# The second transform stage with 128 weight columns per matmul instead of two matmuls of 64

## The chip, the cores and the metric

The kernel runs on one core of a Trainium2 chip. The metric is the device time of one execution, in microseconds (us). Before the change three runs gave 624.28, 624.87 and 624.88 us, median 624.87.

## What is computed

The model is one block with two branches, each behind a layer norm whose scale and shift come from a small conditioning vector. The first branch is a long convolution along the sequence (2048 positions, 512 channels), the second a feed-forward layer with a squared ReLU. Cut to what matters here:

```
K  = real(einsum("dn,dnl,dn->dl", C, exp(dt*A*l), dt*B))   # 512 channels, 2048 taps
Kf = rfft(pad(K, 2048));  Uf = rfft(pad(h.T, 2048))
y  = irfft(Uf * Kf)[:2048].T + h * Dskip
x  = x + ga * y
x  = x + gb * (relu(layernorm(x)*(1+cb)+sb) @ w1 + b1)**2 @ w2 ...
```

The kernel never calls an FFT: both transforms, of the filter K and of the input u, are products with constant matrices, in two stages. The change touches the second of them.

## The kernel before

The 512 channels are cut into 8 chunks of 64 (`NC = 8`), and each chunk passes through the same steps twice, once for the input (lower-case u below) and once for the filter that the kernel generates:

- *Filter generation* (lines around 730 to 805): ScalarE makes sines and exponentials, GpSimd and VectorE multiply them into factors, and TensorE contracts them into a bank called `kg` (line 804, weights of 32 columns).
- *Stage 1* (`stage1`, line 668): a transform of length 32, as matmuls with 64 weight columns and 128 moving columns; the two halves `r` of the output, real and imaginary, go to the two halves of the 128 partitions of a PSUM bank.
- *Stage 2* (`stage2`, line 678): for each of the 32 frequencies k1 a transform of length 64 over the 128 partitions. The weight is `t2_sb[:, k1, r]`, 64 columns for each half r; the moving operand is a strided slice of 64 columns of a 2048-column spectrum tile (called `xy`). One call handles 8 values of k1 and fills one bank `ps`, and one chunk needs four calls. Eight chunks, input and filter, four calls each: 64 calls, 16 matmuls each, 1,024 matmuls in all.
- *Product and first inverse stage* (lines 814, 823, 829): VectorE multiplies the filter's spectrum, straight from the PSUM bank of stage 2, with the input's; TensorE then applies `e1_sb` (64 weight columns, 128 moving).
- *Second inverse stage* (line 1016, weights of 32 by 32), layer norm, and the feed-forward layer (lines 1090 to 1134), whose matmuls have 128 weight columns and 512 moving columns of a rounded 32-bit type.

Every one of these transform matmuls is in plain 32-bit floats, and the profile shows two weight loads and two matmul records for each. So a call of stage 2 leaves 32 records of each kind before the change, in the form 128*64 128x64: weights of 128 rows by 64 columns, 64 moving columns.

The banks `ps` are three, handed round in turn (`PS, XY = 3, 7`). ScalarE empties the input's banks of stage 2 (line 701), and VectorE the filter's (line 814).

The order of the work is not the order of the code. `keep_order` walks all recorded instructions with a model of each engine's time and gives every engine a fixed list. Its time for a plain matmul depends on the number of weight columns:

```python
            tiles = 128 // cols if cols in (32, 64, 128) else 1
            t = max(1.7 * moving / tiles, 116 / tiles)
```

and it adds 100 ns whenever the number of weight columns on TensorE changes from one group to the next. In this model two matmuls of 64 columns with 64 moving columns take 2 x 58 = 116 ns, and so does one of 128 columns. It also keeps a modelled clock of TensorE, and a count of instruction words (`length`, 4 for a plain 32-bit matmul) after which the next block of instructions must have been fetched. Pieces of work also carry hand-set priorities (`HURRY`).

Of the kernel before, what the change touches and what calls it, by code (L numbers as in the profile page):

```python
# [320 lines left out]
def tile_adaln_ssm_ffn(  # L321
# [18 lines left out]
    nc = tc.nc  # L340
# [24 lines left out]
    def bank(tag, bufs, shape=None):  # L365
        n = 1024 if tag == "tg" else 512
        t = ring(psum, tag, bufs, [P, n])
        if shape is None:
            return t
        names = "abcd"[: len(shape) - 1]  # L370
        return t.rearrange(f"p ({' '.join(names)}) -> p {' '.join(names)}", **{x: v for x, v in zip(names, shape[1:])})
# [20 lines left out]
    def held(pool, slot, name, shape, dt=F32):  # L392

        t = pool.tile(shape, dt, tag=slot, name=name)
        slots[t.tensor.name] = slot
        return t
# [19 lines left out]
    def runs(xs):  # L416
        return xs.rearrange("p d m t -> p (d m t)")
# [24 lines left out]
    t2_sb = held(ka, "t2", "t2_sb", [P, 32, 2, 64])  # L442
# [171 lines left out]
    for row_, v in ((g1, g4), (s1, s4)):  # L614
        for q in range(4):
            nc.tensor.matmul(
                row_[:, 128 * q : 128 * q + 128], ident[:, 32 * q : 32 * q + 1].to_broadcast([P, P]), v,
                start=True, stop=True)
# [53 lines left out]
    def stage2(xs, g):  # L672

        ps = bank("ps", PS)
        src = runs(xs).rearrange("p (q k h t) -> p k q h t", q=16, h=2, t=2)
        for i in range(8):
            for r in range(2):
                nc.tensor.matmul(  # L678
                    ps[64 * r : 64 * r + 64, 64 * i : 64 * i + 64].rearrange("p (h q t) -> p q h t", h=2, t=2),
                    t2_sb[:, 8 * g + i, r], src[:, 8 * g + i], start=True, stop=True)  # L680
        return ps.rearrange("p (k h q t) -> p h q k t", k=8, h=2, t=2)


# [11 lines left out]
    def u_pieces(c):  # L695
        xs = xus[c] = spectrum()
        for g in range(4):
            stage1(x_sb[c][:, 4 * g : 4 * g + 4], xs, 4 * g)
            yield
        for g in range(4):  # L700
            nc.scalar.copy(piece(xs, g), stage2(xs, g))
            yield
# [105 lines left out]
    def product_pieces(c):  # L808
        xu, sw, xk = xus[c], sws[c], xks[c]
        yr, yu = spectrum(), spectrum()  # L810
        for g in range(4):
            ps = stage2(xk, g)
            for y, x in ((yr, sw), (yu, xu)):
                nc.vector.tensor_mul(product_piece(y, g), ps, piece(x, g))  # L814
            if g == 3:
                spectra.extend((sw, xu, xk))
            yield
        for g in range(4):
            ps = bank("ps", PS)
            for i in range(4):  # L820
                for h, y in ((0, yu), (1, yr)):
                    for m in range(2):
                        nc.tensor.matmul(  # L823
                            ps[64 * m : 64 * m + 64, 128 * i : 128 * i + 128],
                            pairs(y)[:, g, i // 2, 64 * m : 64 * m + 64, i % 2],
                            e1_sb[:, h], start=(h == 0), stop=(h == 1))
            copy = nc.vector.tensor_copy
            for r in range(2):
                copy(z4[r][c][:, :, 4 * g : 4 * g + 4], ps.rearrange("p (d r j) -> p j d r", d=4, r=2)[..., r])  # L829
            if g == 3:  # L830
                spectra.extend((yr, yu))
            yield
# [493 lines left out]
```

## Time and profile before

| What | Value |
|---|---|
| Median of three runs | 624.87 us |
| Span of the profiled execution | 625.9 us (the page gives no other time for it; 1.0 us over the median) |
| Matmuls busy (PE) | 566.7 us, 9,230 records |
| Weight loads busy (PEld) | 490.4 us, 9,230 records |
| VectorE, ScalarE, GpSimd busy | 485.4, 425.1, 251.7 us |
| Stage 2 (line 678), matmuls | 66.8 us busy, 2,048 records, between 75.7 and 282.6 us of the span |

The columns of a group of instructions are its line, engine and operation, output and inputs by name, the shape of the weights (rows*columns), the shapes of output and moving operand, the count, then busy time in us and the mean duration of one in ns, and then the idle time before them with what ended it. PE rows are matmuls, PEld rows the weight loads that go with them; a matmul's duration includes the passage through the array, so records of one stream overlap, and the distance between their starts is what the stream costs. In the chain of waits each row is a start, a length and the work that the end of the program depended on in that time.

### The profile page before, as it was taken

How to read it: one execution, taken by the hardware profiler on the slowest of the kernel's cores; microseconds unless marked ns; L12 is line 12 of the kernel's file. 1: busy time of each engine (PE TensorE's matmuls, PEld its weight loads, DVE VectorE, ACT ScalarE, POOL GpSimd, SP SyncE). 2: the span in 40 equal slices, each digit the busy share in tenths (PEclk: the TensorE clock that was granted, in tenths of full speed). 3: DMA queues.
4: the chain of work that ended last, by engine and by line, in shares of the span. 5: the costliest groups of instructions: out<-in, count | busy, mean ns of one | idle time of the engine just before them, and what ended most of it. 6: DMA issues, size and time to landing. Idle time of an engine off the chain costs nothing.

```text
span 625.9 us, 21088 instructions
## 1 busy us (share of the span) xinstructions
PE 566.7 (91%) x9230; PEld 490.4 (78%) x9230; DVE 485.4 (78%) x846; ACT 425.1 (68%) x752; POOL 251.7 (40%) x215
## 2 busy tenths in 40 slices
PE   1338999999999999989699899999999999999996
PEld 1236889899899998988578678888888878888885
DVE  3999968798699979835898998646999886655744
ACT  2966879989989677641575866757666766666530
POOL 3849699899998898471004100000000500000000
PEclk9999999999999999999689999999999999999999
DMA  9940231130303303156206421112521532111432
GB/s 319 398 146 3 70 70 31 45 71 3 72 5 71 67 7 71 31 125 225 85 4 214 147 78 34 35 34 85 186 84 45 174 102 72 47 34 35 144 96 79
DMA packets 31355, 57.00 MB, mean 91 GB/s; under 512 B 4512, under 2 KB 13600, under 8 KB 29856
## 3 DMA queue, kind: packets, MB, share of 16 engines
q1 hardware_dynamic: 30832, 55.53, 29.2%
q8 instruction: 72, 1.18, 0.8%
q10 hardware_dynamic: 432, 0.14, 0.1%
q14 instruction: 19, 0.16, 0.1%
HBM read 43.07 MB, written 4.19 MB: 76 GB/s over the span
## 4 chain that ended last, share of the span: by engine, by line
PE 60%; DVE 18%; ACT 12%; DMA 4%; issue 4%; POOL 0%; SPq 0%; DVEq 0%; ACTq 0%
PE ps L668 7%; PE ps L678 7%; PE ps L823 7%; PE kg L804 4%; PE ps L1090 4%; PE ps L1092 3%; PE ps L1094 3%; PE tg L1132 3%; PE tg L1134 3%; PE tg L1133 3%; DMA work<-w 2%; PE ps L1132 2%; PE ps L1134 2%; PE ps L1133 2%; DVE xy L627 2%
## 5 line engine op out<-in xcount | busy, mean ns | idle before, releaser
L951 POOL TENSOR_TENSOR work<-work 128x256 f32<-128x256 f32 x4 | 3.4, 860 | 195.7 <-DMA work<-w 195.6
L925 DVE TENSOR_TENSOR w2t<-rw,w2t 128x512 fp32r<-128x512 f32 x53 | 37.7, 714 | 39.5 <-ACT w2t L924 39.3
L678 PE MATMUL ps<-xy,t_sb 128*64 128x64 f32 x2048 | 66.8, 223 | 1.7 <-issue 0.7
L678 PEld LDWEIGHTS ps<-xy,t_sb 128*64 128x64 f32 x2048 | 63.9, 138 | 3.6 <-issue 1.0
L924 ACT CAST w2t<-rw 128x512 fp32r<-128x512 f32 x53 | 32.8, 619 | 43.9 <-PE kg L1134 24.3
L823 PE MATMUL ps<-e_sb,xy 128*64 128x128 f32 x1024 | 60.8, 273 | 1.2 <-ACT ksb L870 0.7
L1077 ACT ACTIVATE more<-more,b1c 128x512 f32<-128x512 f32 x54 | 38.9, 720 | 28.8 <-DVE more L1115 16.5
L823 PEld LDWEIGHTS ps<-e_sb,xy 128*64 128x64 f32 x1024 | 56.5, 139 | 2.2 <-ACT ksb L870 0.8
L1132 PE MATMUL tg<-w2t,t2t 128*128 128x512 f32 x112 | 44.0, 392 | 0.8 <-DVE t2t L1084 0.7
L670 ACT COPY xy<-ps 128x512 f32<-128x512 f32 x64 | 36.5, 591 | 11.4 <-PE ps L668 11.3
L1133 PE MATMUL tg<-w2t,t2t 128*128 128x512 f32 x112 | 43.6, 389 | 0.0
L1134 PE MATMUL tg<-w2t,t2t 128*128 128x512 f32 x112 | 43.6, 389 | 0.0
L814 DVE TENSOR_TENSOR xy<-ps,xy 128x512 f32<-128x512 f32 x64 | 40.0, 683 | 0.6 <-issue 0.2
L924 ACT CAST wset<-work 128x512 fp32r<-128x512 f32 (+2 forms) x36 | 24.7, 690 | 22.3 <-DMA work<-w 13.7
L760 POOL TENSOR_TENSOR llph<-lo,big 128x1024 int32<-128x1024 int32 x16 | 34.3, 2146 | 10.6 <-ACT tg L772 10.5
L829 DVE COPY big<-ps 128x256 f32<-128x256 f32 x64 | 24.0, 418 | 16.1 <-PE ps L823 16.1
L1090 PE MATMUL ps<-opt,wset 128*128 128x512 f32 x84 | 34.0, 404 | 2.7 <-ACT more L1101 2.7
L668 PE MATMUL ps<-d_sb,ksb 128*64 128x128 f32 x512 | 34.3, 276 | 1.5 <-DVE ksb L871 1.1
L760 POOL TENSOR_TENSOR rtlph<-lo,big 128x1024 int32<-128x1024 int32 x16 | 34.3, 2145 | 3.2 <-ACT tg L772 2.6
L668 PE MATMUL ps<-d_sb,big 128*64 128x128 f32 x512 | 33.1, 274 | 0.7 <-ACT big L634 0.7
L1132 PE MATMUL ps<-w2t,t2t 128*128 128x512 f32 x84 | 33.5, 399 | 0.0
L1092 PE MATMUL ps<-opt,wset 128*128 128x512 f32 x84 | 32.8, 391 | 0.0
(272 smaller groups left out, 1655.7 us busy)
## 6 DMA issues: line engine op xcount, KB each, us to landing
rw<-w SPq DMA_DIRECT2D x53, 256.0 KB, 2.6
xy<-xy SPq DMA_DIRECT2D x16, 512.0 KB, 6.6
xy<-xt SPq DMA_DIRECT2D x24, 256.0 KB, 5.2
xy<-w_mod SPq DMA_DIRECT2D x6, 1024.0 KB, 8.7
work<-w SPq DMA_DIRECT2D x12, 512.0 KB, 4.3
out_dram<-more SPq DMA_DIRECT2D x14, 256.0 KB, 2.0
t_sb<-c_t SPq DMA_DIRECT2D x1, 2048.0 KB, 16.3
i2c<-c_i SPq DMA_DIRECT2D x2, 1024.0 KB, 5.1
```

The source lines that it names most:

```text
L668: nc.tensor.matmul(ps[64 * r : 64 * r + 64, 128 * i : 128 * i + 128], src[:, i], d1_sb[:, r], start=True, stop=True)
L678: nc.tensor.matmul(ps[64 * r : 64 * r + 64, 64 * i : 64 * i + 64].rearrange("p (h q t) -> p q h t", h=2, t=2), t2_sb[:, 8 * g + i, r], src ...
L760: nc.gpsimd.tensor_tensor(ph.rearrange("p d r (a b) -> p (d r) a b", a=4), bc(low_phase[:, us].rearrange("p d r b -> p (d r) b"), 2, 4), b ...
L814: nc.vector.tensor_mul(product_piece(y, g), ps, piece(x, g))
L823: nc.tensor.matmul(ps[64 * m : 64 * m + 64, 128 * i : 128 * i + 128], pairs(y)[:, g, i // 2, 64 * m : 64 * m + 64, i % 2], e1_sb[:, h], st ...
L924: nc.scalar.copy(hi_, raw_)
L1077: nc.scalar.activation(c, c if src is None else src, AF.Relu, bias=b1c[:, t : t + 1])
L1090: pe.append(nc.tensor.matmul(ps, dst[:, 0, wi, kt], o[:, 0, kt], start=start and kt == 0, stop=False, skip_group_check=on))
L1092: pe.append(nc.tensor.matmul(ps, dst[:, 1, wi, kt], o[:, 0, kt], start=False, stop=False, skip_group_check=on))
L1132: nc.tensor.matmul(to[m], l[:, xs], hi_, start=(t == 0), stop=False),
L1133: nc.tensor.matmul(to[m], h[:, xs], lo_, start=False, stop=False),
L1134: nc.tensor.matmul(to[m], h[:, xs], hi_, start=False, stop=(t == NF - 1))])
```

## The change

In `stage2` the inner loop over the halves r goes. One matmul takes both halves as 128 weight columns (they lie side by side in `t2_sb`) and writes all 128 partitions of the bank. What is computed, the weights, the moving operand and the place of each result are the same. The 1,024 matmuls become 512, each twice as wide, with 16 records of each kind per call instead of 32.

```diff
         for i in range(8):
-            for r in range(2):
-                nc.tensor.matmul(
-                    ps[64 * r : 64 * r + 64, 64 * i : 64 * i + 64].rearrange("p (h q t) -> p q h t", h=2, t=2),
-                    t2_sb[:, 8 * g + i, r], src[:, 8 * g + i], start=True, stop=True)
+            nc.tensor.matmul(
+                ps[:, 64 * i : 64 * i + 64].rearrange("p (h q t) -> p q h t", h=2, t=2),
+                t2_sb[:, 8 * g + i].rearrange("p r m -> p (r m)"), src[:, 8 * g + i], start=True, stop=True)
```

The lists of the engines change too, since the model of `keep_order` now sees changes of the column count around each call. In the rows below, `64x16x2x2` or `128x16x2x2` is the output (partitions first), the input names are the source tiles, and a last x16 or x8 counts equal instructions. All later lines are one lower after the change (678 is 677, 804 is 803, 823 is 822).

On TensorE, early in the transform part, where calls of stage 2 (L678) stand between stage 1 (L668) and filter contraction (L804), before:

```order
L678 MATMUL ps_151<-xy_91,t_sb 64x16x2x2 x16
L668 MATMUL ps_152<-d_sb,big_84 64x128 x8
L804 MATMUL kg_351<-llph 32x64 x32
L678 MATMUL ps_151<-xy_93,t_sb 64x16x2x2 x16
L678 MATMUL ps_150<-xy_93,t_sb 64x16x2x2 x16
L668 MATMUL ps_152<-d_sb,ksb_825 64x128 x8
L678 MATMUL ps_150<-xy_91,t_sb 64x16x2x2 x16
L678 MATMUL ps_151<-xy_92,t_sb 64x16x2x2 x16
```

and with the change:

```order
L677 MATMUL ps_150<-xy_91,t_sb 128x16x2x2 x8
L668 MATMUL ps_152<-d_sb,big_84 64x128 x8
L803 MATMUL kg_351<-llph 32x64 x32
L677 MATMUL ps_151<-xy_93,t_sb 128x16x2x2 x8
L677 MATMUL ps_150<-xy_93,t_sb 128x16x2x2 x8
L668 MATMUL ps_152<-d_sb,ksb_825 64x128 x8
L677 MATMUL ps_150<-xy_91,t_sb 128x16x2x2 x8
L803 MATMUL kg_351<-rtlph 32x64 x32
```

Each call is 8 matmuls of 128 output partitions where it was 16 of 64, its neighbours keep 64 or 32, and a group of line 803 has moved ahead of the next call. Over the whole list the number of output partitions changes 85 times from one row to the next before, and 124 times with the change; 40 of the 124 go from a smaller number to 128, and 40 back (10 and 10 of the 85).

On TensorE, at the last calls of stage 2, before:

```order
L678 MATMUL ps_152<-xy_95,t_sb 64x16x2x2 x16
L678 MATMUL ps_150<-xy_95,t_sb 64x16x2x2 x16
L678 MATMUL ps_151<-xy_95,t_sb 64x16x2x2 x16
L823 MATMUL ps_152<-e_sb,xy_94 64x128 x2
L823 MATMUL ps_152<-e_sb,xy_96 64x128 x2
```

and with the change:

```order
L677 MATMUL ps_152<-xy_95,t_sb 128x16x2x2 x8
L677 MATMUL ps_150<-xy_95,t_sb 128x16x2x2 x8
L677 MATMUL ps_151<-xy_95,t_sb 128x16x2x2 x8
L822 MATMUL ps_152<-e_sb,xy_94 64x128 x2
L822 MATMUL ps_152<-e_sb,xy_96 64x128 x2
```

Here nothing but the form of the matmuls differs. From the second inverse stage to the end, TensorE's list holds the feed-forward layer's matmuls in the same order as before.

## The prediction

> **What bounds the kernel now.** I began with the page's slices of the span and its chain of waits, to see whether TensorE is the engine that counts where stage 2 stands.
>
> ```profile
> span 625.9 us, 21088 instructions
> PE 566.7 (91%) x9230; PEld 490.4 (78%) x9230; DVE 485.4 (78%) x846; ACT 425.1 (68%) x752; POOL 251.7 (40%) x215
> PE   1338999999999999989699899999999999999996
> PEclk9999999999999999999689999999999999999999
> PE 60%; DVE 18%; ACT 12%; DMA 4%; issue 4%; POOL 0%; SPq 0%; DVEq 0%; ACTq 0%
> L678 PE MATMUL ps<-xy,t_sb 128*64 128x64 f32 x2048 | 66.8, 223 | 1.7 <-issue 0.7
> L678 PEld LDWEIGHTS ps<-xy,t_sb 128*64 128x64 f32 x2048 | 63.9, 138 | 3.6 <-issue 1.0
> ```
>
> TensorE is 91% busy in all, and at 9 in nearly every slice after the fourth. An average over stages is not enough, so the second view is the busy time of each engine in the stretch that holds every call of stage 2:
>
> ```profile
> core 0: us, PE busy (x) PEld busy (x) DVE busy (x) ACT busy (x) POOL busy (x), PEclk, DMA share, GB/s
> 75.00:283.00 208.00, 202.01 (x5907) 191.61 (x5899) 167.61 (x274) 168.16 (x271) 183.13 (x136) 1.00 0.23 53
> ```
>
> TensorE works 202.0 of 208.0 us there, at the full granted clock, and the next engine, GpSimd, 183.1. An engine that is idle for 6.0 us can hide no more than 6.0 us of further work of its own, whatever the chain says of the other engines. Third, the chain of waits in order of time, which gives the price of each stream undisturbed (columns: start, length, what):
>
> ```profile
> 181.62 2.80 PE ps L678 x96
> 184.42 1.05 PE kg L804 x64
> 185.47 1.02 PE ps L668 x16
> 186.50 0.93 PE ps L678 x32
> 187.43 0.88 PE ps L668 x16
> ...
> 192.25 1.75 PE ps L823 x32
> ...
> 198.36 1.05 PE kg L804 x64
> 199.42 1.90 PE ps L823 x32
> ...
> 282.66 1.81 PE ps L823 x32
> 284.47 1.09 PE ps L918 x8
> 285.56 7.17 PE ps L823 x128
> ```
>
> A call of stage 2 (32 records) takes 0.93 us, or 29.1 ns a record and 116 ns for one k1 (four records). Stage 2's neighbours run with no gap on both sides: this is a saturated TensorE, and 64 x 0.93 = 59.5 us of it is stage 2.
>
> **The change, part by part.** It takes out 512 matmuls and makes 512 others twice as wide. Three things have a price: what a wide record costs, what changing the width costs, and what can hide it.
>
> *Streaming.* A matmul record's duration grows by 53 ns from 64 to 128 moving columns:
>
> ```profile
> L804 PE MATMUL kg<-rtl x704: 216/219/245, 69.9 to 266.8; 128*32 128x64 f32 x176
> L804 PEld LDWEIGHTS kg<-rtl x704: 106/110/111, 69.9 to 266.7; 128*32 128x32 f32 x176
> L678 PE MATMUL ps<-xy,t_sb x2048: 217/222/270, 75.7 to 282.4; 128*64 128x64 f32 x187
> L678 PEld LDWEIGHTS ps<-xy,t_sb x2048: 132/138/138, 75.7 to 282.4; 128*64 128x64 f32 x187
> L918 PE MATMUL ps<-gb,ident x8: 275/275/376, 284.4 to 285.3; 128*128 128x128 f32 x8
> L918 PEld LDWEIGHTS ps<-gb,ident x8: 185/190/192, 284.4 to 285.2; 128*128 128x128 f32 x8
> ```
>
> (275 - 222 = 53 ns). So a record of 64 moving columns streams for about 53 ns, yet records of stage 2 start every 29 ns. The two halves therefore run side by side, each half starting a record every 58 ns. One wide matmul streams its two records one after the other: 2 x 58 = 116 ns for one k1, the same as the two narrow ones now. In streaming nothing is gained and nothing lost.
>
> *Weight loads.* One load lasts 138 ns for 64 columns and 190 ns for 128: 52 ns more for 64 columns, 0.81 ns a column, so that a load would occupy its columns for some 52 ns now and 104 ns with the change. Now the loads start every 29 ns too, since the two halves also load side by side; a wide load covers both halves and has nothing beside it. The nearest rows with plain 32-bit weights of 128 columns are the 8 records of line 918, in order of time (start, length):
>
> ```profile
> 284.40 0.97 PEld L918 LDWEIGHTS ps<-gb,ident 128*128 128x128 f32 x8 [0.17 <-DVE xy L814]
> 284.40 1.16 PE L918 MATMUL ps<-gb,ident 128*128 128x128 f32 x8
> ```
>
> The loads start every (970 - 190)/7 = 111 ns. The stream of their 128 moving columns takes 107 ns as well, so this row bounds the load from above and does not isolate it. From below, a load that never binds leaves the 58 ns of the stream. Bounds for one record: 58 to 111 ns; I take 111, because the form of the weights is line 918's, and the growth of 0.81 ns a column agrees with it. A call then takes 16 x 111 = 1.78 us instead of 0.93, and 64 calls 64 x 0.85 = 54 us more. The lower bound gives 16 x 58 = 0.93 us and no change.
>
> The Trainium skill, TensorE: Matmul & The Clock Gate, section "Back-to-back issue gap", gives about 81 ns as the sustained spacing of load and matmul pairs with 128 moving columns, under what the eight records here show (111 ns). By 81 ns a call would take 1.30 us, and the sum below would come to an estimated 653 us. It is the third of the rivals, the load that hides in part.
>
> *Changes of width.* Counted in the two lists of TensorE, the width changes 85 times before and 124 times after; to 128 columns 10 and then 40 times, back 10 and 40 times, between 32 and 64 the remaining 65 and 44. The chain rows price them. After a group of line 804 (32 columns) 16 records of line 668 take 1.02 us instead of 0.88, and 32 of line 823 1.90 instead of 1.75: 0.14 to 0.15. To 128: 1.09 - 8 x 0.111 = 0.20 us. Back: 7.17 - 4 x 1.75 = 0.17 us. So 60 changes more at 0.18 are 11 us, 21 fewer at 0.14 are -3 us: 8 us more. Bounds: 39 changes more in all at 0.12 (64 records of line 804 at 14.5 ns are 0.93, and 1.05 stand there) are 5 us; 60 at 0.20 are 12 us.
>
> *What hides it.* No other engine can, since the work is TensorE's own and in its order. Its idle 6.0 us in this stretch can shrink, because the engines that it waits for get more time. I count 4 of the 6 as taken up (0 to 6). If none is taken up, the time is 4 us longer. ScalarE at line 701 and VectorE at line 814, who empty stage 2's banks, gain slack and set nothing.
>
> *Instruction words.* 512 matmuls fewer, of four words each by the planner's count, are 2,048 words in blocks of 256: 8 of these blocks fewer. The waits put down to issue before the loads bound their worth:
>
> ```profile
> PEld kg L804 <- issue: 4.8, 19, 1.1
> PE kg L804 <- issue: 1.1, 2, 0.9
> PE ps L678 <- issue: 0.7, 1, 0.7
> ```
>
> On TensorE itself that is 1.8 us, part of the idle 6.0 already counted.
>
> *After stage 2.* From the second inverse stage on, TensorE's list is the same, so 283 to 626 us should move as a block. The lists of the other engines change in the transform part; their mistakes there are covered by a TensorE that is later than the planner thinks.
>
> **The sum.** 54 + 8 - 4 = 58 us on the profiled execution's span of 625.9 us, which is 1.0 us over the median of the runs. On the runs' scale 624.9 + 58 = 683 us. Its own range: with 104 ns a record, 5 us of changes and all 6 us hidden, 16 x 104 = 1.66, 64 x 0.73 = 47, 47 + 5 - 6 = 46: 671. With 12 us of changes, nothing hidden: 54 + 12 = 66: 691.
>
> **The rivals.**
>
> *The load does not bind* (chance 0.07). A load of 128 columns would have to be finished in 58 ns. For it: the transposes, which also load 128 columns, show a short load:
>
> ```profile
> L1046 PEld LDWEIGHTS tg<-ident,more x32: 138/140/142, 438.5 to 464.1; 128*128 128x128 f32 x32
> ```
>
> That is the 138 of 64 plain columns. Against it: the plain 128 columns of line 918 last 190. Then only the width changes remain: 624.9 + 8 - 4 = 629 us, still slower.
>
> *The wide form wins* (0.06), the case on the other side. The load does not bind, and a change of width costs nothing of its own. What line 918 shows as 0.20 us would be its wait for its bank (0.17 <-DVE xy L814, above). The place is each call, and the mechanism that fewer records start: a record's start costs 58 - 53 = 5 ns, which the wide form pays alone; if the stream shrinks to 53 + 2 = 55 ns a record, 64 x 16 x 3 ns = 3 us go, and the issue waits of 1.8 us with them: 624.9 - 5 = 620 us. It decides as soon as a load takes less than 58 ns. Against it: the load's row, and the 0.17 us that line 823 pays after line 918 with no wait shown.
>
> *The load hides in part* (0.07). If a load's own time is its duration less that of the shortest one, 190 - 110 = 80 ns, a call takes 1.28 us: 64 x 0.35 = 22 us, 624.9 + 22 + 8 - 4 = 651 us. For it: nothing isolates the 111 ns. Against it: on this count a load of 32 columns would cost nothing, while the durations grow evenly with the columns, by 28 ns for the second 32 and 52 for the next 64.
>
> *The clock falls as well, or nothing overlaps* (0.07). A call with loads every 111 ns streams for only 53 of them, 48%. The trace shows a full clock with the rows of line 631 at 32 records of 27 ns (107 ns on four groups of columns) each 1.44 us, 60%, and a halved clock once TensorE is nearly idle:
>
> ```profile
> 58.19 1.08 PE L631 MATMUL ps<-xy,ident 128*32 128x128 f32 x32 [0.36 <-DVE xy L627]
> 59.63 1.25 PE L631 MATMUL ps<-xy,ident 128*32 128x128 f32 x32 [0.36 <-DVE xy L627]
> 300.34:303.76 3.42, 0.69 (x33) 0.24 (x18) 3.35 (x10) 1.81 (x3) 0.00 (x0) 0.50 0.56 232
> ```
>
> 48% lies between. The runs of three calls or more, 36 of the 64 calls in the new list, last over 5 us each; were they at half clock for half their time, 18 x 1.78 = 32 us would come on top: 715 us. If loads and matmuls took turns instead (111 + 58 ns), a call would take 2.70 us, and 64 x 1.77 + 4 = 117 us: 742. Line 918 speaks against that: its loads and matmuls together keep 111 ns.
>
> *More of it is hidden* lies inside the forecast's case: the chain puts 30% of the span on VectorE and ScalarE, and a third of 62 us would leave 666. TensorE's 202 of 208 us speak against it.
>
> **How the numbers follow.** Forecast (loads of 111 ns bind): 0.73. Load not binding 0.07, wide form wins 0.06, hidden in part 0.07, clock or no overlap 0.07. The predicted time is the forecast's, 683 us. The range must hold 0.8: the forecast's own 671 to 691, widened for wrong order and clock upwards to 702 and downwards over the partly hidden load to 650; the cases at 620, 629 and 715 or more stay out. A difference under 0.2% (1.2 us) cannot be told from none. Slower: 0.73 + 0.07 + 0.07 + 0.06 = 0.93; faster 0.04 and same 0.03, from the wide form's case and the smallest sizes of the next.
>
> **What would show it.** In the profile after, line 677 has 1,024 records of each kind. If I am right, a call alone takes 1.75 to 1.8 us in the chain, loads of about 190 ns start every 107 to 111 ns, and their busy time is at or over the matmuls'. The stretch from the first to the last call grows from 207 to about 265 us, GpSimd's and VectorE's shares in it fall, and the part after it keeps its 343 us. The width changes are right if the group after a call begins 0.15 to 0.2 us late. A call at 0.93 us proves the load not to bind; a granted clock under 1.00 within the stretch, the fourth rival.

## The result and the profile after

The change makes the kernel slower: 689.23 us (four runs, 686.80 to 692.24) against 624.88, a ratio of 1.101 with a 95% interval of 1.099 to 1.104. That is 64.4 us more; 58 were forecast. The profiled execution took 689.66 us, 1.8 more than its span. Of all the runs behind the figures of this document one, of the kernel with four quarters (705.05 us), fell in a state of lower granted clock, 0.85, and its time is left out.

The page of the changed kernel (engines, slices, instruction queue, the two groups of stage 2):

```profile
span 687.9 us, 19028 instructions
PE 627.8 (91%) x8206; PEld 548.1 (80%) x8206; DVE 490.2 (71%) x846; ACT 427.4 (62%) x752; POOL 250.6 (36%) x215
PE   1358999999989999999987899999999999999997
q8 instruction: 64, 1.05, 0.6%
L677 PE MATMUL ps<-xy,t_sb 128*128 128x64 f32 x1024 | 120.9, 276 | 0.0
L677 PEld LDWEIGHTS ps<-xy,t_sb 128*128 128x128 f32 x1024 | 116.7, 192 | 4.6 <-issue 2.7
```

Half as many records of stage 2 keep TensorE busy for 120.9 us where it was 66.8. The other engines' busy time hardly changes, and their shares fall because the span grows. The engines that empty stage 2's banks now wait for it 60 times (the answer on line 677):

```profile
L677 PEld LDWEIGHTS ps<-xy,t_sb x1024: 186/192/192, 74.6 to 342.5; 128*128 128x128 f32 x171
...
who waited for it (us, times):
  ACT xy L700: 33.2, 30
  DVE xy L813: 30.4, 30
```

The chain of waits, in order of time, has the price of a call:

```profile
140.14 1.02 PE ps L668 x16
141.16 1.93 PE ps L677 x16
143.09 1.90 PE ps L668 x32
144.99 3.72 PE ps L677 x32
...
279.14 9.07 PE ps L677 x80
```

One call after another width takes 1.93 us and two take 3.72, so a call by itself takes 1.79; five in a row take 9.07. That is 16 records of 111 to 112 ns, where 32 records of 29 ns took 0.93. The first call pays some 0.15 us for the new width (1.93 - 1.79), and the group behind it 0.15 again (1.02 where 0.87 stands between equal widths).

The stretch from the first to the last call, as one row of the windows view (columns as in the prediction), for the change:

```profile
74.60:342.80 268.20, 261.66 (x4822) 247.62 (x4820) 171.03 (x272) 169.71 (x270) 183.45 (x136) 0.99 0.18 42
```

and for the kernel before:

```profile
75.70:282.50 206.80, 200.81 (x5848) 190.51 (x5843) 166.41 (x272) 167.46 (x270) 181.93 (x136) 1.00 0.23 52
```

The stretch grows by 61.4 us: TensorE is busy 60.9 us longer, and its idle time is 6.5 us, where it was 6.0. So the mechanism is the forecast one, and yet two things are left over. None of the idle time was taken up, and the granted clock in this stretch is no longer quite full. In windows of 3.41 us (busy time, granted clock, DMA):

```profile
119.45:122.87 3.42, 1.99 (x23) 0.83 0.56 115
122.87:126.28 3.41, 3.41 (x46) 0.67 0.84 195
...
191.13:194.54 3.41, 2.17 (x42) 0.83 0.72 142
194.54:197.95 3.41, 3.41 (x79) 0.67 0.68 171
```

Both falls follow calls of stage 2 (six in a row, then two) and then a gap of over a microsecond in which TensorE waits. In the chain the first one reads:

```profile
119.95 1.43 issue
121.38 8.88 PE ps L822 x128
...
345.81 7.17 PE ps L822 x128
```

The same 128 records take 8.88 us behind the gap and 7.17 later: this fall costs 1.7 us. The second one, in order of time (start, length, idle time before):

```profile
193.81 1.95 PE L803 MATMUL kg<-rtlph 128*32 128x64 f32 x64 [1.24 <-DVE ksb L870]
195.69 1.62 PE L668 MATMUL ps<-d_sb,ksb 128*64 128x128 f32 x16
197.15 1.04 PE L668 MATMUL ps<-d_sb,big 128*64 128x128 f32 x16
```

From start to start the 64 records of line 803 take 1.88 us where 1.05 is usual, and the 16 of line 668 1.46 where it is 1.02: some 1.3 us.

### The profile page after: what moved, and what is told of

Same layout as the page of the kernel before. It is cut to its first block, busy times and chain, and to the rows that moved or that the text cites. A ratio compares the mean times of both kernels' runs of the same rounds, so it can differ in the third digit from the quotient of the medians.

```text
span 687.9 us, 19028 instructions
## 1 busy us (share of the span) xinstructions
PE 627.8 (91%) x8206; PEld 548.1 (80%) x8206; DVE 490.2 (71%) x846; ACT 427.4 (62%) x752; POOL 250.6 (36%) x215
## 3 DMA queue, kind: packets, MB, share of 16 engines
q8 instruction: 64, 1.05, 0.6%
## 4 chain that ended last, share of the span: by engine, by line
PE 71%; DVE 16%; ACT 6%; issue 4%; DMA 2%; SPq 0%; DVEq 0%; ACTq 0%
PE ps L677 17%; PE ps L822 9%; PE ps L668 8%; PE kg L803 5%; PE ps L1089 3%; PE ps L1091 3%; PE ps L1093 3%; PE tg L1131 3%; PE tg L1132 3%; PE tg L1133 3%; PE ps L1133 2%; PE ps L1131 2%; PE ps L1132 2%; DMA work<-w 2%; DVE xy L627 2%
## 5 line engine op out<-in xcount | busy, mean ns | idle before, releaser
L677 PE MATMUL ps<-xy,t_sb 128*128 128x64 f32 x1024 | 120.9, 276 | 0.0
L677 PEld LDWEIGHTS ps<-xy,t_sb 128*128 128x128 f32 x1024 | 116.7, 192 | 4.6 <-issue 2.7
L822 PE MATMUL ps<-e_sb,xy 128*64 128x128 f32 x1024 | 62.6, 279 | 4.0 <-issue 2.2
L813 DVE TENSOR_TENSOR xy<-ps,xy 128x512 f32<-128x512 f32 x64 | 41.4, 686 | 31.6 <-PE ps L677 30.4
L822 PEld LDWEIGHTS ps<-e_sb,xy 128*64 128x64 f32 x1024 | 57.9, 142 | 5.8 <-issue 2.5
L670 ACT COPY xy<-ps 128x512 f32<-128x512 f32 x64 | 36.6, 588 | 30.1 <-PE ps L668 25.2
L700 ACT COPY xy<-ps 128x512 f32<-128x512 f32 x32 | 18.8, 586 | 33.4 <-PE ps L677 33.2
L1089 PE MATMUL ps<-opt,wset 128*128 128x512 f32 x84 | 34.6, 412 | 3.0 <-ACT more L1100 3.0
L668 PE MATMUL ps<-d_sb,ksb 128*64 128x128 f32 x512 | 34.8, 280 | 0.0
L668 PE MATMUL ps<-d_sb,big 128*64 128x128 f32 x512 | 33.2, 276 | 0.7 <-ACT big L634 0.7
```

What stands on the lines that cost most here:

```text
L668: nc.tensor.matmul(ps[64 * r : 64 * r + 64, 128 * i : 128 * i + 128], src[:, i], d1_sb[:, r], start=True, stop=True)
L677: nc.tensor.matmul(ps[:, 64 * i : 64 * i + 64].rearrange("p (h q t) -> p q h t", h=2, t=2), t2_sb[:, 8 * g + i].rearrange("p r m -> p (r m ...
L822: nc.tensor.matmul(ps[64 * m : 64 * m + 64, 128 * i : 128 * i + 128], pairs(y)[:, g, i // 2, 64 * m : 64 * m + 64, i % 2], e1_sb[:, h], st ...
L1089: pe.append(nc.tensor.matmul(ps, dst[:, 0, wi, kt], o[:, 0, kt], start=start and kt == 0, stop=False, skip_group_check=on))
```

## The experiments

The theory: a plain 32-bit load keeps its columns for a time that grows with their number, two halves side by side hide that, and one wide load does not. The rivals: the wide record costs by what it streams or writes; the new lists of the engines cost part of the time; changes of width do.

**The wide form on the old lists, and the narrow form on the new ones.** The planner is misled about stage 2 alone (its column count, and its words so that they count as in the other form), and then every engine's list is the same, instruction by instruction, as in the other kernel.

```diff
+            kind = 64 if second(groups[g]) else kind
-            words = sum(length(i) for i in groups[g])
+            words = sum(length(i) for i in groups[g]) * (2 if second(groups[g]) else 1)
```

For the narrow form it is 128 in place of 64 and half the words in place of twice. `second` is true for groups whose weights are `t2_sb`. Where a kernel below stands on given lists, its planner is misled likewise.

> The wide matmuls of the change, on exactly the lists of instructions that every engine had before (the planner is told that stage 2 still has 64 columns and as many words). Loads that bind: as the change, 689 us (686 to 693), a call of 16 records 1.78 us, since the form alone costs the time. Rival, the new order costs part of it: clearly under the change, 683 or less.

> The narrow matmuls of before, on exactly the lists of instructions of the change. Loads that bind: 625 us (623 to 628), since the order costs nothing by itself. Rival, the new order costs part of the time: 630 or more.

The wide form on the old lists takes 677.94 us, a ratio of 1.086 (1.083 to 1.090): 54.3 us over the kernel before on that chip (623.66). The narrow form on the new lists takes 638.34, 1.024 (1.019 to 1.029): 14.7 us for the order alone. In both the rival named before the run was right. The same stretch, wide on the old lists:

```profile
74.40:335.10 260.70, 258.30 (x4822) 244.56 (x4821) 170.82 (x272) 170.12 (x270) 183.95 (x136) 1.00 0.18 43
```

and narrow on the new ones:

```profile
75.10:291.20 216.10, 202.52 (x5851) 190.47 (x5846) 168.77 (x272) 167.11 (x270) 181.83 (x136) 1.00 0.22 50
```

The form adds 57.5 us of busy time to TensorE and takes its idle time from 6.0 to 2.4 us. The order adds 1.7 us of busy time and takes the idle time from 6.0 to 13.6 us. That is 9.3 us; the spans of the two profiles differ by no more than 9.6 (635.5 and 625.9), so the rest of the 14.7 is not in them. In the waits of TensorE, narrow on the new lists:

```profile
PE ps L828 <- ACT xy L675: 3.0, 3, 1.4
PE ps L673 <- DVE ksb L876: 2.2, 3, 1.2
PE kg L809 <- DVE ksb L876: 2.1, 2, 1.2
```

TensorE stands before banks that ScalarE and VectorE empty too late for it. A slower TensorE hides at most a part of such lateness: with wide matmuls the new lists still cost some 10 us (64.4 - 54.3). The two profiles with wide matmuls differ in the stretch by 4.1 us of idle time (6.5 - 2.4) and 3.4 of busy time (261.66 - 258.30, of which the two falls of the clock make about 3.0). Behind the stretch they differ by 4.3 us (345.1 and 340.8), which is no more than the runs of the change spread (686.80 to 692.24) and is not put down to anything. On the old lists no window of the stretch shows a clock under 1.00.

**Is it the price in the planner, or the one list?** First the change with the planner told the measured price:

```diff
-            t = max(1.7 * moving / tiles, 116 / tiles)
+            t = 222 if second([ins]) else max(1.7 * moving / tiles, 116 / tiles)
```

> The change, with the planner told that a wide matmul takes 222 ns and not 116, which is what the trace of the change shows; the lists come out anew. If the list of the change is bad because it was made for the wrong price, this one comes to the 678 us of the wide form on the old lists, or under. Rival, any list but the one that the hand-set priorities were found for costs some ten microseconds, whatever the prices: 685 to 695 us.

It takes 686.96 us, ratio 1.099 (1.094 to 1.104): no better than the change within the intervals, and 1.2% behind the old lists in ratio. The right price does not mend the list. Then the kernel of before with nothing changed but the planner's price of a change of width, 100 ns:

```diff
-            cost += 100 if kind != shape else 0
+            cost += 110 if kind != shape else 0      # and, in another kernel, 140
```

> The kernel of before with one number of its planner changed: 110 ns for a change of width instead of 100. No instruction differs, only the lists. If the hand-set priorities fit the one list that they were found for, and any other list costs idle time on TensorE in the transform part: 630 to 640 us. Rival, what made the change's list bad is that it avoids changes of width (100 ns for each of 124): so small a step leaves 623 to 628 us.

> The same with 140 ns, which is what a change of width between 32 and 64 columns takes in the trace of before. Priorities that fit one list: 630 to 640 us, no better and no worse than with 110. Rival, a planner with the measured price makes a better list: under 624 us.

633.98 us, ratio 1.011 (1.006 to 1.017), and 632.40, 1.009 (1.005 to 1.013). Ten nanoseconds more in the planner cost as much as 40 more, and both kernels lose, by 6 to 8 us, to the list that the priorities stand for. In both the clock falls once, with narrow matmuls, behind a gap of 2.1 and of 2.0 us; with 140 ns the window behind the gap reads:

```profile
109.90:113.31 3.41, 3.41 (x37) 3.41 (x34) 1.70 (x5) 3.41 (x18) 3.41 (x4) 0.50 0.99 226
```

Five other lists, three with narrow matmuls and two with wide ones, all lose 6 to 15 us against the old list with the same form. Whether the priorities could be found anew for the wide form was not tried.

**The halves one after the other.** Nothing is wide here; each call does the eight matmuls of one half, then those of the other:

```diff
-        for i in range(8):
-            for r in range(2):
+        for r in range(2):
+            for i in range(8):
```

> The narrow matmuls of before, but in each call the eight of the first half and then the eight of the second half, so that neighbours share their columns of the array. Nothing is wide, no width changes more often. If what the change loses is that two halves load and stream side by side: 32 records of 58 ns, a call of 1.86 us, 64 x 0.93 = 59 us more, 684 us (675 to 692). Rival, the wide form itself is dear (128 partitions written, the array set to another width): 625 us.

660.55 us, ratio 1.058 (1.053 to 1.062), on unchanged lists. The chain, and the loads of line 678 in two short windows (start, length, count):

```profile
260.56 7.86 PE ps L678 x160
269.47 6.36 PE ps L678 x128
...
260.60 0.72 PEld L678 LDWEIGHTS ps<-xy,t_sb 128*64 128x64 f32 x11
261.29 0.84 PEld L678 LDWEIGHTS ps<-xy,t_sb 128*64 128x64 f32 x16
```

Five calls take 7.86 us and four 6.36: 1.57 to 1.59 a call, against 0.93 with the halves in turn and 1.86 expected. The same matmuls and the same loads lose 37 us when their neighbours share columns, so the loss needs no wide form. The size was off, though not for the spacing: within a half the loads start every 58 ns, as expected ((720 - 138)/10). Where the half changes, 16 loads take 0.84 us, and at 58 ns they would take 15 x 58 + 138 = 1.01: about three records start beside others. A call has two such changes, and 32 - 5 = 27 records at 58 ns make 1.57 us; that count is an estimate from the two rows.

**Half the loads, the same streaming.** Each weight is loaded once for two k1, with 128 moving columns; every second k1 gets its neighbour's weights, and the columns of a bank stand in another order.

```diff
-        for i in range(8):
-                ... src[:, 8 * g + i], start=True, stop=True)
+        for i in range(0, 8, 2):
+                ... src[:, 8 * g + i : 8 * g + i + 2], start=True, stop=True)
```

> Wide, on the lists of the change, but each weight is loaded for two k1 at once: four matmuls of 128 moving columns a call in place of eight of 64. Every second k1 gets its neighbour's weights, and a bank's columns stand in another order; as many columns are streamed and written as in the change. Loads that bind: 8 records of 111 ns, a call of 0.89 us and the changes of width alone remain: 624.9 + 8 - 3 = 630 us (626 to 636). Rival, the wide record costs by what it streams or writes: a call stays at 1.78 us, 689 us.

636.52 us, ratio 1.020 (1.016 to 1.025). It stands on the lists of the change, so its partner is the narrow form there, 638.34 us, and not the kernel before. The chain:

```profile
242.80 4.66 PE ps L683 x40
```

Five calls take 4.66 us: 0.90 a call with the 0.15 us of the first taken off, 8 records of 112 ns. A load of 128 columns paces its record at 111 to 112 ns with 64 moving columns and with 128 alike, so streaming twice as much for each load was free. With half of the loads gone the changes of width remain, and the kernel is no slower than the narrow form there. In the stretch TensorE is busy 205.93 us, 3.4 more than the narrow form on the same lists, although its 64 calls take 2 us less; one fall of the clock (to 0.51 between 170.8 and 174.2 us) is in it.

**Twice the loads, the same streaming**, wide and narrow: each matmul becomes two of 32 moving columns.

```diff
+            for q in (slice(0, 8), slice(8, 16)):
+                nc.tensor.matmul(to[:, q], <the same weights>, src[:, 8 * g + i, q], start=True, stop=True)
```

> The change on its own lists, with each wide matmul split into two of 32 moving columns: twice the loads, the same streaming. Loads of 128 columns that bind: 32 records of 111 ns, a call of 3.55 us instead of 1.78, 64 x 1.78 = 114 us more, 803 us or a little over if the clock falls more often. Rival, what binds a wide record is what it streams: 689 us.

> The kernel of before on its own lists, with each narrow matmul split into two of 32 moving columns: twice the loads of 64 columns, the same streaming. If a load keeps its columns for 0.83 ns each, it binds here too: 53 to 58 ns a record in each half, 64 records of 27 to 29 ns, a call of 1.75 to 1.86 us, 675 to 683 us. Rival, a load of 64 columns hides behind less streaming: 16 ns a record, a call of 1.0 us, 630 us.

Wide, one run took 964.53 us, 162 over the 803 expected. The call at full clock is as expected, and a second price stands beside it (the slices of the granted clock, the answer on its line, and the chain):

```profile
PEclk9997855585875775765855787579999999999999
L685 PEld LDWEIGHTS ps<-xy,t_sb x2048: 186/333/338, 75.0 to 618.6; 128*128 128x128 f32 x187
...
212.33 6.97 PE ps L685 x32
...
255.92 3.69 PE ps L685 x32
```

At full clock a call takes 3.69 us, 0.15 and 32 records of 111 ns, as expected. But in most of the stretch the slices show a mean clock of 0.5 to 0.8, and where it is down the load lasts 333 ns instead of 190, and the call 6.97 us. Here a record streams some 27 of 111 ns, 24% (half of the 53 that 64 columns take). The loads start as densely as in the change, where seven calls in a row kept a full clock on the old lists, so in these runs time spent on loads does not hold the clock; and loads slow down with it. TensorE's rows alone would not show it (two windows of that stretch, busy time and granted clock):

```profile
80.50:94.10 13.60, 13.60 (x81) 13.54 (x82) 2.49 (x4) 2.99 (x5) 6.47 (x4) 0.50 0.01 1
125.00:175.00 50.00, 50.00 (x342) 0.53 0.01 1
```

Narrow, one run took 693.26 us:

```profile
256.28 1.84 PE ps L686 x64
279.17 9.46 PE ps L686 x320
```

A call between equal widths takes 1.84 us, and five behind another width 9.46: 64 records a call, 29 ns a record with the halves side by side. That is the spacing of before, 58 ns in a half, with half the streaming, so the load of 64 columns does bind, at 58 ns. The whole is 10 us over the expected upper end, and its granted clock falls twice in the stretch.

**Four quarters of 32 columns**, the opposite of the change, on the old lists:

```diff
-            for r in range(2):
+            for m in range(4):   # ps[32 * m : 32 * m + 32], the weights' columns 32 * m to 32 * m + 31
```

> The opposite of the change: four matmuls of 32 weight columns for each k1, side by side on four groups of columns, on the lists of before. Loads and streams of all groups side by side: 64 records of 14.5 ns as in the filter contraction, a call of 0.93 us as before, with 79 changes of width in place of 85: 624 us (621 to 628). Rival, a record's start costs something that doubles with the number of records, or the doubled words are not fetched in time: 630 or more.

(The 79 is a miscount: the lists hold 105 changes of width with this form.) 675.23 us (three runs, 674.05 to 677.36), ratio 1.081 (1.077 to 1.086). The expectation missed by 51 us, for the most part for its rival's second reason (the page, a window of the stretch, and the chain):

```profile
q8 instruction: 88, 1.44, 0.9%
L684 PE MATMUL ps<-xy,t_sb 128*32 128x64 f32 x4096 | 72.4, 224 | 22.2 <-issue 21.3
74.40:331.20 256.80, 216.53 (x7910) 198.61 (x7900) 182.19 (x273) 184.58 (x270) 191.52 (x136) 0.97 0.19 45
...
267.99 2.00 PE ps L684 x128
```

Where it is undisturbed, two calls take 2.00 us, 0.14 of it for the width: 0.93 a call, as expected. But 88 blocks of instructions come instead of 72, and TensorE is idle for 40.3 us of the stretch (256.80 - 216.53) where it was 6.0. The matmuls of this line alone wait 21.3 us for "issue", in 20 pieces of about a microsecond. That these waits are the fetch of instructions is inferred from the count of blocks and not shown otherwise. TensorE is also busy 15.7 us longer (216.53 - 200.81) at a mean clock of 0.97, which is not taken apart here.

## Why the prediction was right, and where not

*TensorE bounds the stretch, and nothing can hide its work*: right. On equal lists 57.5 us more of busy time became 54.3 us of run time.

*Streaming, no gain and no loss*: right for a call of wide records with halved loads (0.90 us) and of quarters (0.93). The 53 ns were read wrongly, from a difference of durations: wide records last 275 ns with 64 moving columns too, and narrow ones 222 ns with 32 as with 64. The size stands by another row of the prediction: 32 records of line 823, two halves side by side with 128 moving columns, take 1.75 us, 109 ns a record in each half, and by estimate half of that for 64 columns. The 58 ns of before are not the stream's alone: loads of 64 columns keep to them with half the streaming (narrow, twice the loads).

*The load, 54 us*: right, and the value taken (111 ns, the upper bound) was the true one. The wide record keeps 111 to 112 ns with 32, 64 and 128 moving columns, so the row of line 918, which could not tell load from stream, was showing the load. Each record has one load, so another cost of each record that grows with its weight columns is not told apart from the load itself. The Trainium skill, TensorE: Matmul & The Clock Gate, section "LDWEIGHTS (loading the stationary operand)", puts a load at its columns over 1.2, in ns, which is 107 for 128 columns; the trace, at 111 to 112 ns, agrees within 5%. The 81 ns of the Trainium skill, TensorE: Matmul & The Clock Gate, section "Back-to-back issue gap", is not what these 32-bit loads do (111 ns with 128 moving columns).

*Changes of width, 8 us*: the right kind, a little too large. Measured 0.15 us on each side (0.20 and 0.17 were taken): 60 x 0.15 - 21 x 0.14 = 6 us; the busy time on equal lists leaves 57.5 - 54.4 = 3, and why the two differ stays open. The Trainium skill, TensorEngine Tiling (Array Packing), section "Key Properties", says that a change of tiling mode drains the engine. A change of width costs 0.15 us here; that a drain is the reason no run shows.

*Four of six idle microseconds are taken up*: right on the old lists (3.6), and wrong for the change, where nothing was.

*"Their mistakes there are covered by a TensorE that is later than the planner thinks"*: wrong, and this is the step that failed. The lists cost 14.7 us with narrow matmuls and some 10 with wide ones. Two terms (the hidden idle time and this zero) were too kind, one (the width) a little too hard, and so 58 came out under 64. The total came near because its largest term, the load, was right; that the errors of the small ones partly offset each other is luck.

*The part behind keeps its 343 us*: nearly. It is 345.1 us with the change (687.9 - 342.8) and 340.8 with the wide form on the old lists (675.9 - 335.1).

*The clock rival*: by the sign that the prediction set for it, a granted clock under 1.00 in the stretch, it came in, with two falls and some 3.0 us in place of its 32. The 48% alone do not bring a fall: on the old lists seven calls in a row, 12.66 us, keep a full clock. Both falls stand behind a gap; but gaps of 1.1 us at 92 and 272 us leave the clock of the change full, and with narrow matmuls gaps up to 1.8 us do so on the new lists, while gaps of 2.0 and 2.1 us bring a fall with the planner at 140 and 110 ns. So it is not shown how much the wide calls have to do with the two falls. At 24% no gap is needed: the clock falls 5.5 us after the first call, with TensorE busy all the time.

## What to carry to other kernels

Where a matmul moves few columns, ask for the load's own time before its stream's: here two narrow halves loaded at once, and a wide load of the same weights took twice as long (111 ns, where each half had 58). Test that by changing the number of loads and not the streaming. And where a tuned planner sets the order, run the new form on the old lists and the old form on the new ones: any other list cost 1 to 2.4% here, which would otherwise have been put down to the form.

## What the runs showed beside that

Narrow stage 2 stood at two limits at once: loads of 64 columns keep their half for 58 ns with half the streaming, and records of 64 moving columns keep to 58 ns with loads of 32 columns (the quarters, 14.5 ns a record on four groups). One step to more records of smaller width ran into a third, 40.3 us of idle time on TensorE, most of it put down to issue. And the granted clock did not follow TensorE's busy time: with streaming at 24% it fell to 0.53 in a window where TensorE was busy all the time by its rows, so a busy row is no sign of a held clock.
